# Key and query weights transposed by the DMA queues instead of TensorE, and late loads moved to GpSimd's queue

## The chip, the cores and the metric

The kernel runs on one core of a Trainium2 chip. The core has a matrix engine (TensorE, PE in the profile; its weight loads are listed as PEld), VectorE (DVE), ScalarE (ACT), GpSimd (POOL) and SyncE (SP), which here only issues transfers. Sixteen DMA engines move data between HBM and the on-chip memory SBUF; they are fed by queues that SP, ScalarE and GpSimd issue into. Matmul results go to PSUM, eight banks of 512 fp32 columns. The metric is the time of one execution on the device in microseconds (us); lower is better.

## The reference

A layer norm feeds two branches, which are added to the input: linear attention with a softmax feature map (32 heads of 16), and a gated feed-forward layer with GELU.

```python
# x: 1 x 2048 x 512, H = 32, Dh = 16, feed-forward width 1376, all bf16
def _A_ref(x, wqkv, w_phi, wo):
    qkv = (x @ wqkv) ...                      # split into q, k, v per head
    pq = einsum("bhsd,hdf->bhsf", q, w_phi)
    pk = einsum("bhsd,hdf->bhsf", k, w_phi)
    phi_q = concat([softmax(pq), softmax(-pq)])
    phi_k = concat([softmax(pk), softmax(-pk)])
    kv = einsum("bhsf,bhsd->bhfd", phi_k, v)
    z  = einsum("bhsf->bhf", phi_k)
    num = einsum("bhqf,bhfd->bhqd", phi_q, kv)
    den = einsum("bhqf,bhf->bhq", phi_q, z) + 1e-6
    return (num / den) ... @ wo
def _B_ref(x, w_gate, w_up, w_down):
    return (gelu(x @ w_gate) * (x @ w_up)) @ w_down
xn = layernorm(x)
return x + _A_ref(xn, ...) + _B_ref(xn, ...)
```

## The kernel before

**Tiling.** The 2048 tokens are 16 tiles of 128 (index t or r) and 4 chunks of 512 (index s). The normed input is kept transposed in `xnT`, channels on the partitions. The feed-forward width is 11 units (`NF`; ten of 128 and one of 96), index jf; `J = s*11 + jf`.

**Who decides the order.** Every instruction is first put down as an operation with its reads, writes and a cost in us (`op`, `alt`, `dma`). A list scheduler (`Sched.schedule`) then walks a model of the engines, always takes the ready operation with the lowest priority number, and so fixes one order per engine. That order is replayed with semaphore waits in front of each operation (`_replay`). On the chip an engine never goes past a waiting instruction: what stands behind it in the order waits too. A DMA belongs to the engine that issues it, so a DMA that waits for something stops that engine: SP, or GpSimd in the middle of its arithmetic. SP has 12 DMA semaphores and uses them in turn.

**The stages.**

1. Start: 11 spare matmuls on zeros, then token tiles 0 to 3: `ln_stats`, `ln_rstd` (on GpSimd) and `ln_norm` on VectorE write `xn_sb` (six buffers); `xt_pe` transposes them on TensorE, and `gate4` starts the gate projection of chunk 0.
2. Feed-forward chunk 0: for each unit, gate and up projections (`lin`, four 512-wide matmuls each, into banks 0 to 3), GELU on ScalarE and the product with up on VectorE (`glu`, into `hT`). The norms of tiles 4 to 7, 8 to 11 and 12 to 15 (`ln_group`) run beside it on VectorE, and `xt_dma` transposes each by a DMA that SP issues, SBUF to SBUF, into `xnT`.
3. Weight folding, also beside chunk 0: the key weights are loaded into a free part of `hT` (`wk_nat`), the query weights into a free part of `EqT` (`wq_nat`). `wtrans` transposes them in four groups of eight 128x128 TensorE transposes through PSUM, `wtrans_out` copies them to SBUF on ScalarE (`wkT`, `wqT`), and `fold` multiplies them with the block-diagonal `bd` made from `w_phi`, giving `wk2` and `wq2`. So pq and pk come straight from xn.
4. Projection phase over 16 token tiles: `proj_k` and `proj_q` (banks 0 to 2 in turn) with two exponentials each on ScalarE, into `Ek` and `EqT`; `proj_v` (banks 3 and 4). The sums of the exponentials, `Ssum`, are made by GpSimd in four steps (`st1`, `st2`, `st3`, `Ssum`), and by VectorE for tiles 3, 7, 11 and 15. `v_post` (VectorE) takes the reciprocal of the sums and scales the values; `kv_acc` (TensorE, "kv product of tile t" below) accumulates key features times scaled values in banks 5 to 7.
5. Chunks 1 to 3 of the feed-forward layer, with the attention (`att`) and the output tiles (`outp`, which uses `wo_sb` and `wd_sb`) in between.

**Loads.** SP issues nearly all of them, in the order: x tiles, gate and up weights, key weights, x 8 to 11, query weights, x 12 to 15, value weights. `gate_dma` is a list of transfers that a load has to wait for. `big_loads` issues wo and w_down from GpSimd, and waits for the last `xnT` transpose (`d_xt[15]`).

Of the kernel before, what the change touches and what calls it, by code (L numbers as in the profile page):

```python
# [7 lines left out]
ACTF = mybir.ActivationFunctionType  # L8
# [40 lines left out]
class Sched:  # L49
# [150 lines left out]
def bass_parallel_sum__linear_kernel_hedgehog__glu_gated_geglu__prompt_kernel(  # L200
# [14 lines left out]
    with ExitStack() as es, nc.allow_low_precision("bf16 softmax factors"):  # L215
# [10 lines left out]
        ident = sb([P, 128], bf16, "ident")  # L226
# [23 lines left out]
        wkT = hT[:, 1, 0:4, :]  # L250
        wk_nat = hT[:, 1, 4:8, :]
# [10 lines left out]
        wqT = EqT[:, 0:4, 1536:2048]  # L262
        wq_nat = EqT[:, 4:8, 1536:2048]
# [25 lines left out]
        def bank16(b):  # L289
            return bank(b).bitcast(bf16)  # L290
# [29 lines left out]
        B_wkn = bufs("wkn", 2)  # L320
        B_wqn = bufs("wqn", 2)
        B_wk2 = bufs("wk2", 4)
        B_wq2 = bufs("wq2", 4)
        B_wv = bufs("wv", 2)
# [25 lines left out]
        def load_x(q, t, n):  # L350
            return dma(q, lambda e: e.dma_start(
                x_all[:, t:t + n, :], x2[t * P:(t + n) * P, :].rearrange("(n p) c -> p n c", p=P)),
                writes=B_x[t:t + n], lat=1.9, kb=128 * n, prio=-900, extra=gate_dma)

        def load_w(dst, lo, bf, qs=("sp", "act")):
            v = A_wqkv[:, lo:lo + 512].rearrange("(i p) c -> p i c", p=P)
            for h, q in enumerate(qs):
                dma(q, lambda e, h=h: e.dma_start(dst[:, 2 * h:2 * h + 2, :], v[:, 2 * h:2 * h + 2, :]),
                    writes=[bf[h]], lat=1.9, kb=256, prio=-900, extra=gate_dma)

        def load_f(dst, src, c, bf, qs=("sp", "act")):
# [17 lines left out]
        dma("pool", lambda e: e.dma_start(  # L379
            wphi[:], A_w_phi.rearrange("(j hl) d f -> (hl d) j f", j=4)), writes=[B_wphi], cost=1.0, lat=4.0,  # L380
            prio=-900)
        load_x("sp", 8, 4)
        load_w(wq_nat, 0, B_wqn, ("sp", "sp"))
        load_x("sp", 12, 4)
        load_w(wv_sb, 1024, B_wv, ("sp", "sp"))


        op("dve", lambda e: e.memset(warm[:], 0.0), writes=[B_warm], cost=0.3, prio=-900)
# [51 lines left out]
        def proj_k(t, b):  # L440
            op("pe", [lambda e, i=i: e.matmul(  # L441
                bank(b), xnT[:, i, t * P:(t + 1) * P], wk2[:, i, :], start=(i == 0), stop=(i == 3))
                for i in range(4)], reads=[B_xnT[t]] + B_wk2, writes=[BK[b]], cost=mm(4))
            for sig in range(2):
                exps.append(op("act", lambda e, sig=sig: e.activation(  # L445
                    Ek[:, t, sig, :], bank(b), ACTF.Exp, scale=(1.0, -1.0)[sig]),
                    reads=[BK[b]], writes=[B_Ek[t][sig]], cost=0.55, extra=gelus, tab="exp"))
            ev = Ek[:, t, :, :].rearrange("p s (h f) -> p (s h) f", f=DH)
            if t in SDVE:
                op("dve", lambda e: e.tensor_reduce(Ssum[:, t, :], ev, axis=mybir.AxisListType.X, op=ALU.add),  # L450
                   reads=B_Ek[t], writes=[B_S[t]], cost=1.24)
# [8 lines left out]
            op("pool", lambda e: e.tensor_tensor(v3, v2[:, :, 0:2], v2[:, :, 2:4], op=ALU.add),  # L460
               reads=[B_st[1]], writes=[B_st[2]], cost=0.4, lock=True)
            op("pool", lambda e: e.tensor_tensor(Ssum[:, t, :], v3[:, :, 0], v3[:, :, 1], op=ALU.add),  # L462
               reads=[B_st[2]], writes=[B_S[t]], cost=0.29)
# [169 lines left out]
                   reads=[B_y[y], B_x[t]], writes=[B_ob[k]], cost=1.17, lock=True)  # L633
            dma("sp", lambda e: e.dma_start(out2[t * P:(t + 1) * P, :], ob[:, k, :]), reads=[B_ob[k]], writes=[], lat=1.3, kb=128)

        def wtrans(w, Bw, jj, b):
            op("pe", [lambda e, i=i, j=j: e.transpose(  # L637
                bank16(b)[:, (j % 2) * 512 + i * 128:(j % 2) * 512 + (i + 1) * 128],
                w[:, i, j * 128:(j + 1) * 128], ident[:]) for j in (2 * jj, 2 * jj + 1) for i in range(4)],
               reads=Bw + [B_ident], writes=[BK[b]], cost=mm(8, 128))  # L640

        def wtrans_out(wT, BwT, jj, b, extra=()):
            dst, src = wT[:, 2 * jj:2 * jj + 2, :], bank16(b).rearrange("p (j c) -> p j c", j=2)
            op("act", lambda e: e.activation(dst, src, ACTF.Copy), cost=1.0, reads=[BK[b]],
               writes=BwT[2 * jj:2 * jj + 2], extra=extra)

        def fold(wT, BwT, w2, B_w2, j, b):
            op("pe", [lambda e, i=i: e.matmul(  # L648
                bank(b)[:, i * 128:(i + 1) * 128], wT[:, j, i * 128:(i + 1) * 128], bd[:, j, :],
                start=True, stop=True) for i in range(4)], reads=[BwT[j], B_bd], writes=[BK[b]], cost=mm(4, 128))  # L650
            dst, src = w2[:, :, j * 128:(j + 1) * 128], bank(b).rearrange("p (i c) -> p i c", i=4)
            alt([("act", lambda e: e.activation(dst, src, ACTF.Copy), 0.55),
                 ("dve", lambda e: e.tensor_copy(dst, src), 0.69)], reads=[BK[b]], writes=[B_w2[j]])


        op("pe", [lambda e: e.matmul(bank(7), warm[:, 0:128], warm[:], start=True, stop=True) for _ in range(11)],  # L656
           reads=[B_warm], writes=[BK[7]], cost=4.2)
# [13 lines left out]
        def kq():  # L671
            turn[0] += 1
            return (turn[0] - 1) % 3
# [38 lines left out]
        for jf in range(4, NF):  # L712
            gelus.append(ffn(jf))
            if jf in (5, 8):
                ln_group({5: 8, 8: 12}[jf])
            if jf in (5, 6):
                wtrans(wk_nat, B_wkn + B_hT[1][4:8], jf - 5, 4 + jf % 2)
                wtrans_out(wkT, B_wkT, jf - 5, 4 + jf % 2)
            if jf in (7, 8):
                wtrans(wq_nat, B_wqn + B_Eq[3][4:8], jf - 7, 4 + jf % 2)  # L720
                wtrans_out(wqT, B_wqT, jf - 7, 4 + jf % 2)
            if jf == 7:
                for j in range(4):
                    fold(wkT, B_wkT, wk2, B_wk2, j, 6 + j % 2)
            if jf == 9:
                for j in range(4):
                    fold(wqT, B_wqT, wq2, B_wq2, j, 6 + j % 2)
        big_loads()


        LAG, KA = 3, 3
        nv = 0

        def val():
# [91 lines left out]
```

## Time and profile before

| | |
|---|---|
| three runs | 201.5, 201.76, 202.19 us (median 201.76) |
| profiled execution | 201.5 us, of which the span of its instructions is 199.7 |
| granted TensorE clock | 1.00 in every stretch |
| TensorE transposes of the weights (L637) | 4 groups of 8, first start 18.55 us |
| DMA transposes into xnT (L425) | 12, first issue 16.9, last issue 35.5 us; 2.4 to 6.7 us to landing |
| first use of wo (L616) | 91.1 us |

The span is counted from the first instruction to the last; all places in time below are from its start. Most of the kernel is the same stream of 512-wide matmuls; the change touches what happens in the first 60 us. DMA traffic by the page, in 40 slices of 5 us:

```profile
GB/s 167 333 377 346 187 103 60 61 299 86 0 0 0 3 0 0 0 28 28 26 53 53 31 53 26 26 49 33 26 26 56 26 30 51 26 54 28 53 26 54
```

The loads of x and of the weights fill the first five slices; the slices at 40 and 45 us are wo and w_down. In what follows a row of a timeline is: start, length, engine and line, operation, tiles, count, and in brackets the idle time before it and who ended it. A length covers all instructions that the row merges.

### The profile page before, as it was taken

The page shows a single profiled execution, that of the slowest core. Times are in us where ns is not written, and L with a number is a line of the kernel's source. Part 1 is how long each engine was busy: PE and PEld are TensorE (multiplying, and loading weights), DVE is VectorE, ACT ScalarE, POOL GpSimd, SP SyncE. Part 2 cuts the span into 40 slices and gives each one's busy share as a digit, 9 for nine tenths or more (in the row PEclk, how much of TensorE's full clock was granted, in tenths as well). Part 3 has the DMA queues.
Part 4 walks back from the last instruction along what each step waited for, and adds up shares of the span by engine and source line. Part 5 has one row for each costly group of instructions (what it writes and reads, how often), then busy time and mean ns, then how long its engine had stood idle before and what let it go on. Part 6 is the DMA issues. An engine that isn't in the chain of part 4 may idle for free.

```text
span 199.7 us, 3131 instructions
## 1 busy us (share of the span) xinstructions
PE 195.3 (98%) x1183; PEld 101.2 (51%) x1183; DVE 130.6 (65%) x297; ACT 81.4 (41%) x140; POOL 75.5 (38%) x105
## 2 busy tenths in 40 slices
PE   7999999999999999999999999999999999999994
PEld 2665665546555556555455555545545555454441
DVE  3788993549868576685986874959167494853121
ACT  2373798985676765343022222322223132222000
POOL 5630212999997820022432242342222324222100
PEclk9999999999999999999999999999999999999999
DMA  5999954282000000011022121041102102021101
GB/s 167 333 377 346 187 103 60 61 299 86 0 0 0 3 0 0 0 28 28 26 53 53 31 53 26 26 49 33 26 26 56 26 30 51 26 54 28 53 26 54
DMA packets 24079, 14.41 MB, mean 72 GB/s; under 512 B 15888, under 2 KB 23584, under 8 KB 24064
## 3 DMA queue, kind: packets, MB, share of 16 engines
q1 hardware_dynamic: 22944, 11.74, 23.7%
q0 software_dynamic: 560, 1.95, 2.9%
q10 hardware_dynamic: 560, 0.52, 0.8%
q8 instruction: 9, 0.15, 0.3%
q14 instruction: 6, 0.05, 0.1%
HBM read 8.44 MB, written 2.10 MB: 53 GB/s over the span
## 4 chain that ended last, share of the span: by engine, by line
PE 98%; DVE 0%; ACT 0%; issue 0%
PE ps_all L536 36%; PE ps_all L620 19%; PE ps_all L616 7%; PE ps_all L466 7%; PE ps_all L477 7%; PE ps_all L441 7%; PE ps_all L568 4%; PE ps_all L503 4%; PE ps_all L656 2%; PE ps_all L551 2%; PE ps_all L637 1%; PE ps_all L648 1%; PE ps_all L433 1%; DVE ob L626 0%; ACT xnT L437 0%; PE ps_all L664 0%
## 5 line engine op out<-in xcount | busy, mean ns | idle before, releaser
L536 PE MATMUL ps_all<-xnT,wu_sb 128*128 128x512 bf16 (+1 forms) x176 | 44.4, 379 | 0.0
L527 ACT ACTIVATE gs<-ps_all 128x512 bf16<-128x512 f32 (+1 forms) x44 | 25.9, 598 | 40.6 <-PE ps_all L536 37.7
L536 PE MATMUL ps_all<-xnT,wg_sb 128*128 128x512 bf16 (+1 forms) x160 | 40.7, 379 | 0.0
L620 PE MATMUL ps_all<-wd_sb,hT 128*128 128x512 bf16 (+1 forms) x176 | 40.6, 379 | 0.0
L608 POOL TENSOR_TENSOR o_sb<-otmp 128x512 bf16<-128x512 bf16 x16 | 18.4, 1153 | 55.6 <-DVE otmp L602 55.6
L529 DVE TENSOR_TENSOR hT<-gs,ps_all 128x512 bf16<-128x512 bf16 (+1 forms) x44 | 28.7, 679 | 14.5 <-PE ps_all L536 14.4
L620 PEld LDWEIGHTS ps_all<-wd_sb,hT 128*128 128x128 bf16 (+1 forms) x176 | 17.2, 98 | 20.8
L536 PEld LDWEIGHTS ps_all<-xnT,wu_sb 128*128 128x128 bf16 (+1 forms) x176 | 17.4, 100 | 19.0
L632 POOL TENSOR_TENSOR ob<-y_sb,x_all 128x512 bf16<-128x512 f32 x12 | 13.8, 1153 | 26.2 <-ACT y_sb L630 26.2
L630 ACT ACTIVATE y_sb<-ps_all 128x512 f32<-128x512 f32 x12 | 7.2, 597 | 40.0 <-PE ps_all L620 40.0
L536 PEld LDWEIGHTS ps_all<-xnT,wg_sb 128*128 128x128 bf16 (+1 forms) x160 | 15.3, 100 | 14.4
L602 DVE TENSOR_TENSOR otmp<-ps_all,cf 128x384 bf16<-128x384 f32 (+1 forms) x48 | 21.7, 507 | 0.5
L487 DVE TENSOR_TENSOR vs<-ps_all,vs 128x1024 bf16<-128x1024 f32 x16 | 19.4, 1217 | 3.4 <-PE ps_all L477 3.2
L445 ACT ACTIVATE Ek<-ps_all 128x512 bf16<-128x512 f32 x32 | 17.3, 610 | 8.1 <-PE ps_all L441 8.0
L472 ACT ACTIVATE EqT<-ps_all 128x512 bf16<-128x512 f32 x32 | 17.7, 619 | 5.1 <-PE ps_all L466 5.1
L585 DVE RECIPROCAL r_sb<-ps_all 128x48 f32<-128x48 f32 (+1 forms) x32 | 9.2, 327 | 13.5 <-PE ps_all L568 13.5
L484 DVE RECIPROCAL vs<-Ssum 128x64 bf16<-128x64 f32 x16 | 8.7, 554 | 12.3 <-POOL Ssum L462 12.2
L466 PE MATMUL ps_all<-xnT,wq 128*128 128x512 bf16 x64 | 16.4, 379 | 0.0
L616 PE MATMUL ps_all<-wo_sb,oT 128*128 128x512 bf16 x64 | 16.4, 379 | 0.0
L477 PE MATMUL ps_all<-wv_sb,xnT 128*128 128x512 bf16 x64 | 16.3, 379 | 0.0
L441 PE MATMUL ps_all<-wk,xnT 128*128 128x512 bf16 x64 | 16.1, 379 | 0.0
L456 POOL TENSOR_TENSOR st<-Ek 128x512 f32<-128x512 bf16 x12 | 13.9, 1154 | 5.3 <-ACT Ek L445 5.3
(64 smaller groups left out, 186.1 us busy)
## 6 DMA issues: line engine op xcount, KB each, us to landing
out_dram<-ob SPq DMA_DIRECT2D x16, 128.0 KB, 1.7
x_all<-in_A_x_dram SPq DMA_DIRECT2D x3, 512.0 KB, 9.8
wd_sb<-in_B_w_down_dram POOLq DMA_DIRECT2D x1, 1280.0 KB, 9.4
wg_sb<-in_B_w_gate_dram SPq DMA_DIRECT2D x2, 432.0 KB, 6.6
wu_sb<-in_B_w_up_dram SPq DMA_DIRECT2D x2, 432.0 KB, 7.7
wu_sb<-in_B_w_up_dram SPq DMA_DIRECT2D x2, 256.0 KB, 4.5
hT<-in_A_wqkv_dram SPq DMA_DIRECT2D x2, 256.0 KB, 8.6
EqT<-in_A_wqkv_dram SPq DMA_DIRECT2D x2, 256.0 KB, 9.6
```

What stands on the lines that cost most here:

```text
L441: op("pe", [lambda e, i=i: e.matmul(bank(b), xnT[:, i, t * P:(t + 1) * P], wk2[:, i, :], start=(i == 0), stop=(i == 3)) for i in range(4)] ...
L466: op("pe", [lambda e, i=i: e.matmul(bank(b), wq2[:, i, p * 128:(p + 1) * 128], xnT[:, i, s * 512:(s + 1) * 512], start=(i == 0), stop=(i = ...
L472: exps.append(op("act", lambda e, g=g, sig=sig: e.activation(EqT[:, g, s * 512:(s + 1) * 512], bank(b), ACTF.Exp, scale=(1.0, -1.0)[sig]), ...
L477: op("pe", [lambda e, i=i: e.matmul(bank(b), xnT[:, i, t * P:(t + 1) * P], wv_sb[:, i, :], start=(i == 0), stop=(i == 3)) for i in range(4 ...
L487: op("dve", lambda e: e.tensor_tensor(v[:, :, :, 0:DH], bank(b).rearrange("p (h d) -> p h d", d=DH).unsqueeze(1).to_broadcast([P, 2, 32, DH]),
L527: h = op("act", lambda e: e.activation(gs[0:w, k, :], bank(gb)[0:w, :], ACTF.Gelu_apprx_tanh), reads=[BK[gb]], writes=[B_gs[k]], cost=0.55 ...
L529: op("dve", lambda e: e.tensor_tensor(hT[0:w, s % 2, jf, :], gs[0:w, k, :], bank(ub)[0:w, :], op=ALU.mult), reads=[B_gs[k], BK[ub]], write ...
L536: op("pe", [lambda e, i=i: e.matmul(bank(b)[0:w, :], wt[:, i, jf * 128:jf * 128 + w], xnT[:, i, s * 512:(s + 1) * 512], start=(i == 0), st ...
L602: op("dve", lambda e, q=q, n=n: e.tensor_tensor(otmp[:, k, q * 384:q * 384 + n * 128].rearrange("p (s h d) -> p s h d", s=n, d=DH), bank(4 ...
L608: op("pool", lambda e: e.tensor_tensor(o_sb[:, k, :], otmp[:, k, 0:512], otmp[:, k, 512:1024], op=ALU.add), reads=B_ot[k], writes=[B_o[k]] ...
L616: fns = [lambda e, j=j: e.matmul(bank(b), oT[:, t % NOT, j, :], wo_sb[:, j, :], start=(j == 0), stop=False) for j in range(4)]
L620: fns.append(lambda e, jf=jf, w=w: e.matmul(bank(b), hT[0:w, s % 2, jf, tl * 128:(tl + 1) * 128], wd_sb[0:w, jf, :], start=False, stop=(jf ...
```

## The change

- `wtrans` no longer makes TensorE transposes; it has SP issue four DMA transposes per weight matrix (128x512 each, SBUF to SBUF), straight into `wkT` or `wqT`. `wtrans_out` is gone. The key weights' four are put down ahead of the norms of tiles 4 to 7, the query weights' four after them. Their priority places all eight on SP ahead of the xnT transposes of tiles 8 to 15.
- `fold` waits for all four DMA transposes of its matrix. The key folds use banks 4 to 7 and follow unit 7 of chunk 0. The query folds are moved from behind unit 9 into the projection phase, behind the first three `proj_k` (`KA` = 3, `FQ` = True).
- The query weights are loaded ahead of x 8 to 15. x 8 to 11, x 12 to 15 and the value weights are now issued by GpSimd: x 8 to 11 after the first half of the second part of the up weights has landed, the others after x 8 to 11 have landed.

```diff
-        load_x("sp", 8, 4)
         load_w(wq_nat, 0, B_wqn, ("sp", "sp"))
-        load_x("sp", 12, 4)
-        load_w(wv_sb, 1024, B_wv, ("sp", "sp"))
+        gate_dma = [B_wu[2].last_write]
+        load_x("pool", 8, 4)
+        gate_dma = [B_x[8].last_write]
+        load_x("pool", 12, 4)
+        load_w(wv_sb, 1024, B_wv, ("pool", "pool"))
...
-        def wtrans(w, Bw, jj, b):
-            op("pe", [lambda e, i=i, j=j: e.transpose(...) for j in (2 * jj, 2 * jj + 1) for i in range(4)],
-               reads=Bw + [B_ident], writes=[BK[b]], cost=mm(8, 128))
-        def wtrans_out(wT, BwT, jj, b, extra=()):
-            op("act", lambda e: e.activation(dst, src, ACTF.Copy), cost=1.0, reads=[BK[b]], ...)
+        def wtrans(w, Bw, wT, BwT):
+            for i in range(4):
+                dma("sp", lambda e, i=i: e.dma_start_transpose(wT[:, :, i * 128:(i + 1) * 128], w[:, i, :]),
+                    reads=[Bw[i // 2]] + Bw[2:], writes=[BwT[i]], cost=1.2, lat=1.4, kb=310)
...
         def fold(wT, BwT, w2, B_w2, j, b):
-            ... reads=[BwT[j], B_bd], writes=[BK[b]], cost=mm(4, 128))
+            ... reads=BwT[0:4] + [BwT[4 + j], B_bd], writes=[BK[b]], cost=mm(4, 128))
...
+        wtrans(wk_nat, B_wkn + B_hT[1][4:8], wkT, B_wkTi)
         ln_group(4)
+        wtrans(wq_nat, B_wqn + B_Eq[3][4:8], wqT, B_wqTi)
...
-            if jf in (5, 6):
-                wtrans(wk_nat, ...); wtrans_out(wkT, ...)
-            if jf in (7, 8):
-                wtrans(wq_nat, ...); wtrans_out(wqT, ...)
             if jf == 7:
                 for j in range(4):
-                    fold(wkT, B_wkT, wk2, B_wk2, j, 6 + j % 2)
-            if jf == 9:
+                    fold(wkT, B_wkTi + B_wkT, wk2, B_wk2, j, 4 + j)
+            if jf == 9 and not FQ:
...
         for r in range(KA):
             proj_k(r, kq())
+        if FQ:
+            for j in range(4):
+                fold(wqT, B_wqTi + B_wqT, wq2, B_wq2, j, (6, 7, 4, 5)[j])
```

As built, SP's order after the loads is: four transposes of the key weights, xnT 4 to 7, four of the query weights, xnT 8 to 15. In GpSimd's order the wo and w_down loads, which wait for xnT 15, now stand between the second and the third step of the sum of token tile 2 (before: between the first and second step of tile 1). TensorE's order in the projection phase begins k0, k1, v0, k2, the query folds, k3, k4, v1, q0, q1, kv 0, v2, k5, q2, kv 1, k6, q3, v3, k7, q4, k8, kv 2, v4, kv 3, q5, v5, kv 4.

More of the change, by code (lines that the diff above doesn't have):

```diff
@@ L320, in bass_parallel_sum__linear_kernel_hedgehog__glu_gated_geglu__prompt_kernel @@
         B_wkn = bufs("wkn", 2)
+        B_wkTi, B_wqTi = bufs("wkTi", 4), bufs("wqTi", 4)
         B_wqn = bufs("wqn", 2)
@@ L634, in outp @@
             dma("sp", lambda e: e.dma_start(out2[t * P:(t + 1) * P, :], ob[:, k, :]), reads=[B_ob[k]], writes=[], lat=1.3, kb=128)
-        def wtrans(w, Bw, jj, b):
-            op("pe", [lambda e, i=i, j=j: e.transpose(
-                bank16(b)[:, (j % 2) * 512 + i * 128:(j % 2) * 512 + (i + 1) * 128],
-                w[:, i, j * 128:(j + 1) * 128], ident[:]) for j in (2 * jj, 2 * jj + 1) for i in range(4)],
-               reads=Bw + [B_ident], writes=[BK[b]], cost=mm(8, 128))
-        def wtrans_out(wT, BwT, jj, b, extra=()):
-            dst, src = wT[:, 2 * jj:2 * jj + 2, :], bank16(b).rearrange("p (j c) -> p j c", j=2)
-            op("act", lambda e: e.activation(dst, src, ACTF.Copy), cost=1.0, reads=[BK[b]],
-               writes=BwT[2 * jj:2 * jj + 2], extra=extra)
+        def wtrans(w, Bw, wT, BwT):
+            for i in range(4):
+                dma("sp", lambda e, i=i: e.dma_start_transpose(wT[:, :, i * 128:(i + 1) * 128], w[:, i, :]),
+                    reads=[Bw[i // 2]] + Bw[2:], writes=[BwT[i]], cost=1.2, lat=1.4, kb=310)
         def fold(wT, BwT, w2, B_w2, j, b):
@@ L649, in fold @@
                 bank(b)[:, i * 128:(i + 1) * 128], wT[:, j, i * 128:(i + 1) * 128], bd[:, j, :],
-                start=True, stop=True) for i in range(4)], reads=[BwT[j], B_bd], writes=[BK[b]], cost=mm(4, 128))
+                start=True, stop=True) for i in range(4)], reads=BwT[0:4] + [BwT[4 + j], B_bd], writes=[BK[b]], cost=mm(4, 128))
             dst, src = w2[:, :, j * 128:(j + 1) * 128], bank(b).rearrange("p (i c) -> p i c", i=4)
@@ L653, in fold @@
                  ("dve", lambda e: e.tensor_copy(dst, src), 0.69)], reads=[BK[b]], writes=[B_w2[j]])
+        LAG, KA, FQ = 3, 3, True
         op("pe", [lambda e: e.matmul(bank(7), warm[:, 0:128], warm[:], start=True, stop=True) for _ in range(11)],
@@ L715, in bass_parallel_sum__linear_kernel_hedgehog__glu_gated_geglu__prompt_kernel @@
                 ln_group({5: 8, 8: 12}[jf])
-            if jf in (5, 6):
-                wtrans(wk_nat, B_wkn + B_hT[1][4:8], jf - 5, 4 + jf % 2)
-                wtrans_out(wkT, B_wkT, jf - 5, 4 + jf % 2)
-            if jf in (7, 8):
-                wtrans(wq_nat, B_wqn + B_Eq[3][4:8], jf - 7, 4 + jf % 2)
-                wtrans_out(wqT, B_wqT, jf - 7, 4 + jf % 2)
             if jf == 7:
                 for j in range(4):
-                    fold(wkT, B_wkT, wk2, B_wk2, j, 6 + j % 2)
-            if jf == 9:
+                    fold(wkT, B_wkTi + B_wkT, wk2, B_wk2, j, 4 + j)
+            if jf == 9 and not FQ:
                 for j in range(4):
-                    fold(wqT, B_wqT, wq2, B_wq2, j, 6 + j % 2)
+                    fold(wqT, B_wqTi + B_wqT, wq2, B_wq2, j, 6 + j % 2)
         big_loads()
-        LAG, KA = 3, 3
         nv = 0
```

## Prediction, made before the changed kernel was run

> **What bounds the kernel now.** I read the page's shares first, then the chain that ended last, then the timelines of each engine over the first 60 us, the only stretch where the diff acts.
>
> ```profile
> PE 195.3 (98%) x1183; PEld 101.2 (51%) x1183; DVE 130.6 (65%) x297; ACT 81.4 (41%) x140; POOL 75.5 (38%) x105
> PE 98%; DVE 0%; ACT 0%; issue 0%
> ```
>
> TensorE is busy for 98% of the span and is 98% of the chain. So a TensorE instruction taken away is worth its full spacing, and a pause put into TensorE costs its full length.
>
> ```profile
> 15.10 1.03 PE L536 MATMUL ps_all<-xnT,wg_sb 128*128 128x512 bf16 x4
> 18.55 0.61 PE L637 MATMUL ps_all<-ident,hT 128*128 128x128 bf16 x8
> 19.00 1.03 PE L536 MATMUL ps_all<-xnT,wg_sb 128*128 128x512 bf16 x4
> 30.76 2.75 PE L441 MATMUL ps_all<-wk,xnT 128*128 128x512 bf16 x12
> ```
>
> Columns: start, length, engine and line, then the work. Eight transposes take 19.00-18.55 = 0.45 us of TensorE, and none of these rows has an idle note. By 15.10 TensorE starts unit 4 of chunk 0; at 30.76 it starts the key projections.
>
> ```profile
> 7.38 1.00 SPq L358 DMA_DIRECT2D hT<-in_A_wqkv_dram  x2
> ...
> 16.95 6.22 SPq L425 DMA_TRANSPOSE xnT<-xn_sb  x4
> 24.37 6.03 SPq L425 DMA_TRANSPOSE xnT<-xn_sb  x4
> 31.62 5.12 SPq L425 DMA_TRANSPOSE xnT<-xn_sb  x4
> 35.52 1.21 SPq L425 DMA_TRANSPOSE xnT<-xn_sb  x1
> DMA to landing us min/median/max: 8.0/8.6/9.3
> ```
>
> This is SP's timeline; the last line is the landing time of the two key-weight loads (first row), so the first half lands at 7.38+8.0 = 15.4. Three of the last four transposes take 5.12-1.21 = 3.91 us, that is, SP issues one DMA transpose per 1.30 us. Each lands 2.43 us after its issue (the smallest of the twelve, 2.4 to 6.7).
>
> ```profile
> 38.26 0.85 POOL L687 DMA_DIRECT2D wo_sb<-in_A_wo_dram  x1
> 39.11 0.98 POOL L690 DMA_DIRECT2D wd_sb<-in_B_w_down_dram  x1
> 40.08 0.56 POOL L693 DMA_DIRECT2D wd_sb<-in_B_w_down_dram  x1
> ...
> 41.47 0.40 POOL L460 TENSOR_TENSOR st<-st 128x128 f32<-128x128 f32 x1
> 41.95 0.29 POOL L462 TENSOR_TENSOR Ssum<-st 128x64 f32<-128x64 f32 x1
> ```
>
> GpSimd issues the wo and w_down loads itself, between two steps of a softmax sum. They wait for the last xnT transpose (35.52+2.43 = 37.95), which in this kernel is there when GpSimd arrives.
>
> ```profile
> 45.04 0.56 DVE L484 RECIPROCAL vs<-Ssum 128x64 bf16<-128x64 f32 x1 [0.94 <-POOL Ssum L462]
> 45.63 2.36 DVE L487 TENSOR_TENSOR vs<-ps_all,vs 128x1024 bf16<-128x1024 f32 x2
> 47.91 1.21 DVE L450 TENSOR_REDUCE Ssum<-Ek 128x64 f32<-128x1024 bf16 x1
> 49.03 0.55 DVE L484 RECIPROCAL vs<-Ssum 128x64 bf16<-128x64 f32 x1
> 49.62 1.23 DVE L487 TENSOR_TENSOR vs<-ps_all,vs 128x1024 bf16<-128x1024 f32 x1
> ```
>
> VectorE waits for GpSimd's sum of token tile 2, and then works 49.62+1.23-45.04 = 5.81 us without a gap until the value tile 4 is scaled. TensorE's kv product of tile 4 needs that tile.
>
> **The change part by part.** *Removed:* 32 transposes on TensorE, 4 groups of 0.45 us (0.445 unrounded), together **-1.78 us**, all on the chain. Four ScalarE copies (1.02 us each) go too; TensorE never waits for ScalarE in these rows, so they are worth nothing.
>
> *Without any new wait* TensorE would go: 15.10 + 7 units of 1.73 (eight 512-wide matmuls, from 19.00 to the next group's start at 20.73) = 27.2; key folds 0.89 (two groups of eight, 0.445 each); then, in the order that the changed kernel is built with, 21 projections of 0.864, the query folds 0.89 and four kv products of 0.475 before the kv product of tile 4: 27.2+0.89+18.14+0.89+1.90 = **49.0**. (0.864 is half of 1.73; 0.475 is the step from a kv product, 66.10, to what follows, 66.57.) The same walk puts the key folds at 22.0, the query folds at 31.5, kv 0 at 36.8 and kv 2 at 45.5.
>
> *Added:* eight DMA transposes on SP, all in the same queue as the twelve of xnT: four of the key weights first, then xnT 4 to 7, four of the query weights, xnT 8 to 15. The first one waits for the key load, 15.4. Before, the last of the twelve started at 35.52; now twenty in a row, bound by SP. The twentieth starts no earlier than 15.4 + 19 x 1.30 = 40.1 and lands at 42.5. Three unknowns stand beside this. The pace: with every start-to-start at the shortest pair seen, 1.23, landing is at 41.3. A hiccup: the middle four took 6.03 us instead of 5.12, so +0.9, and over twenty issues I count one. A full queue: the first four took 6.22 us under the loads, +1.1; if the fifth is not taken until the first has landed, and that comes as late as 25 (before: 16.95+6.7 = 23.6, behind the value weights), the slip is 25-22 = 3; bounds 0 and 3, I take 0.5, half of the 1.1, as only the value weights and x 12 to 15 are left beside them. Landing: 42.5+0.9+0.5 = **43.9**, bounds 41.3 and 46.4.
>
> [...] The rows give 1.30 us of issue each, and the sum goes by them.
>
> *The wait and what stands behind it.* GpSimd's order now has the wo load, still waiting for the last xnT transpose, between the second and third step of the sum of tile 2. GpSimd gets there at about 38 to 40, and stands until 43.9. Behind it: 0.1 to wake, 2.40 for three issues (38.26 to 40.66), 0.77 for two steps of the sum (41.47 to 42.24): tile 2's sum is done at 43.9+3.3 = 47.2, not before 42. VectorE's five instructions take 5.81, with 0.1 for semaphores: kv 4 can start at 53.1, that is **4.1 late**. (kv 2, after reciprocal and product, 1.9 us: 49.1 against 45.5, 3.6 late.) From there sums come every 2.77 us (42.20 to 44.96 before) for three tiles in four, and TensorE needs 3.07 per tile (63.04 to 66.10), so nothing later is later still.
>
> *Other new waits* end on the same TensorE, so the largest counts and not the sum. Key folds: fourth key transpose, start 19.3, landing 21.7 at best and 25 if starved, 0 to 3 late. Query folds: twelfth transpose, 15.4+11x1.30+2.43+1.4 = 33.5 against 31.5, 2.0 late. kv 0: VectorE stands in order at the norm of tile 15 until xnT 9 has freed its buffer, 15.4+13x1.30+2.43+1.4 = 36.1; plus norm 0.4, reciprocal and product 1.9, 38.4 against 36.8, 1.6 late. All are below 4.1.
>
> *Moved:* x 8 to 15 and the value weights to GpSimd's queue, three loads later by a wait each. x 8 starts when the up weights land (13.5). The bytes are the same, and the page's slices from 10 to 20 us already run at 377 and 346 GB/s, so x 8 lands near 18 to 20, against 18.7. VectorE's products for TensorE stand behind it, at most 1 us late, again below 4.1. wo and w_down land near 56 (43.9+2.4+9.4, the longest landing of the three before); the first use is at 91: hidden.
>
> **Sum.** +4.1-1.78 = +2.3. The profiled execution took 201.5 us (span 199.7), the lowest of 201.5, 201.76 and 202.19; 201.5+2.3 = 203.8 by it, 204.1 by the median. Forecast **203.9**. With the bounds of the landing: 41.3 gives 1.5-1.78, so 201.2; 46.4 gives 6.6-1.78, so 206.3.
>
> A pause matters twice if the clock falls. Every stretch here has a granted clock of 1.00 and no pause. [...]
>
> **Rivals.** (a) *Forecast:* SP's chain of twenty holds GpSimd; 202.2 to 205.2. For: the fixed order and 1.30 us. Chance 0.61.
> (b) *Starved transposes:* the software queue's loads keep the key transposes back to 25, the queue fills, landing at 46: 201.5-1.78+46.1-39.8 = 206.0. For: the 6.7 us landing; against: fewer loads than before. 0.15.
> (c) *No change:* no hiccup and no slip, landing 41.0 to 42.2, lateness 1.2 to 2.4 against 1.78 saved: about 201.5. Against: 1.23 was the shortest pair, never a run. 0.14.
> (d) *Faster, the other side:* the twenty land before anybody asks, and only the 1.78 remains: 199.7. Lateness is landing minus 39.8, so it decides from a landing below 41.0 (0.3% off) and is whole at 39.8, at a pace of 1.16. For: 8 x 1.30 us is little against 1183 matmuls; against: the shortest single issue is 1.19. 0.10.
>
> A difference of 0.3%, 0.6 us, is what this kernel's measurement can tell. Below -0.3% is (d), 0.10; within, (c), 0.14; above, (a) and (b), 0.76. Range 201.3 to 206.0: (c), (a) and most of (b); (a)'s own is 202.2 to 205.2.
>
> **What would show it.** Right: no transposes on TensorE; twenty SP transposes at 1.3 us from 15.4 to about 41; GpSimd idle near 39 to 44, released by a DMA into xnT; TensorE idle some 4 us between 22 and 54, last at a kv product. Wrong: GpSimd not idle there, TensorE unbroken, transposes closer than 1.2 us, or a granted clock below 1.

## The result, and the profile after

| | before | after |
|---|---|---|
| median of the runs | 201.95 us (201.5 to 202.19, 4 runs) | 204.64 us (204.53 to 205.48, 4 runs) |
| profiled execution, of which span | 201.5, 199.7 us | 204.53, 202.8 us |
| TensorE transposes of the weights | 32 | 0 |
| first idle note of TensorE after 15 us | none | 23.20 us, four in all |
| last matmul starts at | 196.40 us | 199.23 us |

The ratio is 1.0145, with a 95% interval of 1.0111 to 1.0178: the change costs 2.7 us. The granted clock is 1.00 in every stretch up to the last matmul. Four executions of the experiments below (205.63 to 210.08 us) ran at a lower granted clock (0.983 to 0.992), and the medians and ratios leave them out.

The page's shares and its chain that ended last, after the change:

```profile
PE 193.5 (95%) x1151; PEld 99.0 (49%) x1151; DVE 131.3 (65%) x298; ACT 77.3 (38%) x135; POOL 78.7 (39%) x109
PE 77%; DMA 10%; DVE 5%; SPq 4%; POOL 2%; issue 1%
```

TensorE is busy 193.5 us instead of 195.3, so the 1.8 us of transposes did go. But the chain is 77% TensorE, where it was 98%: the rest passes through SP's queue (SPq), transfers (DMA), GpSimd and VectorE. TensorE's timeline, the rows with an idle note between 15 and 54 us:

```profile
23.20 1.07 PE L645 MATMUL ps_all<-bd,hT 128*128 128x128 bf16 x16 [1.03 <-DMA hT<-hT]
39.29 0.65 PE L506 MATMUL ps_all<-vs,Ek 128*128 128x136 bf16 x8 [1.18 <-DVE vs L490]
49.61 0.65 PE L506 MATMUL ps_all<-vs,Ek 128*128 128x136 bf16 x8 [1.43 <-DVE vs L490]
53.60 0.59 PE L506 MATMUL ps_all<-vs,Ek 128*128 128x136 bf16 x7 [0.28 <-DVE vs L490]
```

In the order of time these are the key folds, released by a transpose of the key weights, and the kv products of token tiles 0, 2 and 4, released by VectorE. The notes come to 3.9 us. A note counts from the modelled end of the matmul before it, some 0.16 us late; from start to start the four cost 1.20, 1.34, 1.60 and 0.44, together 4.6 us. SP's timeline, and below it the summary of the line that issues the xnT transposes (durations, then landing times):

```profile
15.36 5.20 SPq L641 DMA_TRANSPOSE hT<-hT  x4
20.66 5.24 SPq L428 DMA_TRANSPOSE xnT<-xn_sb  x4
25.95 5.41 SPq L641 DMA_TRANSPOSE EqT<-EqT  x4
31.45 11.56 SPq L428 DMA_TRANSPOSE xnT<-xn_sb  x8
```

```profile
L428 SPq DMA_TRANSPOSE xnT<-xn_sb x12: 1210/1260/2430, 20.7 to 41.7; - x12
...
DMA to landing us min/median/max: 2.5/3.4/5.5
```

Twenty transposes in a row keep SP issuing without a break: the first at 15.36, the last at 41.74. The median one takes 1.26 us, one took 2.43, and from start to start it is about 1.3 in most places. The chain of waits, walked back by the profile from TensorE's work at 56 us and shown in the order of time (start, length, what):

```profile
23.20 1.07 PE ps_all L645 x16
...
32.76 4.30 DMA xnT<-xn_sb
37.06 0.03 issue
37.09 0.41 DVE xn_sb L422
...
41.74 2.53 DMA xnT<-xn_sb
44.27 0.29 issue
44.56 0.83 POOL wo_sb L685
45.39 0.00 issue
45.39 0.96 POOL wd_sb L688
46.35 0.55 POOL wd_sb L691
...
47.41 0.30 POOL Ssum L465
...
48.33 2.36 DVE vs L490 x2
...
53.60 0.65 PE ps_all L506 x8
```

It reads: the twentieth transpose is issued at 41.74 and lands at 44.27; only then does GpSimd get past the wo load, which takes it with the two w_down loads to 46.9; only then the sum of tile 2; then VectorE's chain; then TensorE. How long GpSimd and VectorE stood is in their own timelines:

```profile
44.56 0.83 POOL L685 DMA_DIRECT2D wo_sb<-in_A_wo_dram  x1 [4.51 <-DMA xnT<-xn_sb]
47.73 0.56 DVE L487 RECIPROCAL vs<-Ssum 128x64 bf16<-128x64 f32 x1 [5.18 <-POOL Ssum L465]
```

GpSimd idle for 4.51 us in front of a load that nobody needs before 94 us, and VectorE idle for 5.18 us behind it.

From the kv product of tile 15 on, TensorE runs the same stream in both kernels: it starts at 81.03 before and at 83.86 after, and from there to the last matmul both take 115.38 us. So the change is over at about 54 us, and its price there is 83.86-81.03 = 2.83 us: 1.78 saved, 4.61 late. The span grew by 3.04. The remaining 0.2 lies behind the last matmul (3.34 us before, 3.56 after).

### The profile page after: what moved, and what is told of

Same layout as the page of the kernel before. It is cut to its first block, busy times and chain, and to the rows that moved or that the text cites. A ratio compares the mean times of both kernels' runs of the same rounds, so it can differ in the third digit from the quotient of the medians.

```text
span 202.8 us, 3076 instructions
## 1 busy us (share of the span) xinstructions
PE 193.5 (95%) x1151; PEld 99.0 (49%) x1151; DVE 131.3 (65%) x298; ACT 77.3 (38%) x135; POOL 78.7 (39%) x109
## 4 chain that ended last, share of the span: by engine, by line
PE 77%; DMA 10%; DVE 5%; SPq 4%; POOL 2%; issue 1%
PE ps_all L539 31%; PE ps_all L623 19%; PE ps_all L619 7%; PE ps_all L480 5%; PE ps_all L469 4%; PE ps_all L444 4%; PE ps_all L571 4%; DMA hT<-in_A_wqkv_dram 4%; DMA xnT<-xn_sb 3%; PE ps_all L506 3%; DVE vs L490 2%; DMA hT<-hT 2%; SPq L641 2%; SPq L366 2%; DMA x_all<-in_A_x_dram 1%
```

## The experiments

Four runs use the kernel's own DMA transposes. In the other eight every DMA transpose is an ordinary copy of the same 128 KB between the same tiles. They leave the transposition out and keep the numbers and sizes of the rest, so that the pace of the issues can be set apart from the transposing. The start of an execution shifts its places by some 1 us (unit 4 of chunk 0 starts at 14.90 us with the paced copies below and at 15.92 with all waits moved and copies at their own pace); where runs are compared, it is by the time from unit 4 of chunk 0 to the kv product of tile 15, which is 65.93 us in the kernel before (15.10 to 81.03) and 68.76 in the changed one (15.10 to 83.86). Each ratio is to runs of the kernel before on the same chip (medians 202.0, 201.81 and 202.11 us).

**The output weights' loads on SP.** If GpSimd's standing is the price, another issuer for the three loads takes it away and leaves the transposes as they are.

```diff
 def big_loads():
-    dma("pool", lambda e: e.dma_start(wo_sb[:], ...), cost=1.0, ...)
-    dma("pool", ... wd_sb ...)   # twice
+    dma("sp", lambda e: e.dma_start(wo_sb[:], ...), cost=0.8, ...)
+    dma("sp", ... wd_sb ...)     # twice
```

> The changed kernel, with the wo and w_down loads issued by SP behind the last xnT transpose, and not by GpSimd. Theory (GpSimd stands at these loads until 44.3 and keeps the sums of tile 2 and later back): GpSimd's 4.5 us idle and the pauses before kv 2 and kv 4 (1.43 and 0.28 us) go. What is left is TensorE's lateness at kv 0, 39.29 against 36.75 = 2.5, less the 1.78 saved: 0.8 us above before, about 202.7 against 201.95, ratio 1.004; last pause on TensorE at kv 0. Rival (the twenty transposes and the loads of the software queue slow the core by themselves, the place of the wait is incidental): no gain, 204.5, ratio 1.013.

202.70 us, ratio 1.0030 [1.0011, 1.0049], 1.94 us less than the changed kernel. SP's and TensorE's rows of this run:

```profile
44.33 0.39 SPq L685 DMA_DIRECT2D wo_sb<-in_A_wo_dram  x1
```

```profile
24.42 1.04 PE L539 MATMUL ps_all<-xnT,wu_sb 128*128 128x512 bf16 x4 [0.26 <-DVE hT L532]
31.14 1.04 PE L480 MATMUL ps_all<-wv_sb,xnT 128*128 128x512 bf16 x4 [0.51 <-DVE hT L532]
39.23 0.65 PE L506 MATMUL ps_all<-vs,Ek 128*128 128x136 bf16 x8 [0.97 <-DVE vs L490]
42.30 0.64 PE L506 MATMUL ps_all<-vs,Ek 128*128 128x136 bf16 x8
45.36 0.64 PE L506 MATMUL ps_all<-vs,Ek 128*128 128x136 bf16 x8
48.43 0.64 PE L506 MATMUL ps_all<-vs,Ek 128*128 128x136 bf16 x8
```

The twentieth transpose lands at 44.3, as late as before the edit, and still the kv products now follow each other every 3.06 us without a pause. A late transpose by itself cost TensorE nothing there; the load waiting on GpSimd did. From unit 4 to the kv product of tile 15 it is 66.43 us (15.30 to 81.73), 2.33 less than in the changed kernel; only 0.26 of this was gained ahead of kv 0. The three pauses left come to 2.24 us from start to start (1.74 by the notes), which is more than the gain of 1.78.

**The early pauses out, GpSimd left as it is.** Ten layer-norm buffers for six (VectorE no longer stands at tile 15), and the key folds one unit later. A sum of all pauses as the price would make this faster by about 2 us; the largest one alone would hide the others.

```diff
-NXN = 6
+NXN = 10
...
-            if jf == 7:      # key folds
+            if jf == 8:
```

> The changed kernel with ten buffers for the normed tiles in place of six (VectorE needn't stand until xnT 8 and 9 have freed one) and the key folds one unit later. So the two early pauses of TensorE, 1.03 and 1.18 us, lose their cause; GpSimd's wait for the last transpose stays. Theory (waits on one engine count by the largest lateness, not by their sum): the early pauses shrink to 0.3 or less and come back before kv 2, which grows from 1.43 to 3.5 to 4.1 us, as tile 2's sum still comes at 47.7; kv 4 now has a projection more in front of it, so its 0.3 to 0.5 goes. Time 204.1 to 204.6, ratio 1.011 to 1.013. Rival (each pause has its own price): 1.03 + 1.18 less, 202.4, ratio 1.002. [...]

204.53 us (202.84, 204.53 and 204.62), ratio 1.0101 [1.0055, 1.0146]. The median is that of the changed kernel, as it should be if the last wait swallows the early ones. The profile fell on the shortest of the three, whose 202.84 us by itself would also suit the rival. But in it SP's twenty issues had no long one, the twentieth transpose landed at 43.09 and kv of tile 2 started at 48.42, against 44.27 and 49.61 in the changed kernel: 5.33 and 5.34 us behind the landing. The earlier landing (1.18 us) and the pause before kv 4 that is gone (0.44) make 1.6 of the 1.69 us between the two profiled executions. The key folds still waited 0.36 us by the note, kv 0 no longer did, and the pause before kv 2 grew to 1.68, not to the 3.5 to 4.1 expected. The other two executions have no profile, so that their landing was as late as in the changed kernel is not shown.

**The moved loads alone.** The kernel before, with x 8 to 15 and the value weights on GpSimd's queue as in the change.

```diff
-load_x("sp", 8, 4); load_w(wq_nat, ...); load_x("sp", 12, 4); load_w(wv_sb, 1024, B_wv, ("sp", "sp"))
+load_w(wq_nat, ...)
+gate_dma = [B_wu[2].last_write]; load_x("pool", 8, 4)
+gate_dma = [B_x[8].last_write];  load_x("pool", 12, 4); load_w(wv_sb, 1024, B_wv, ("pool", "pool"))
```

> The kernel before with one part of the change: the query weights ahead of x 8 to 15, and x 8 to 15 and the value weights issued by GpSimd behind their waits. The TensorE transposes stay. Theory (the bytes are the same and these loads have slack): x 8 lands near 19.5 and x 12 near 24, twelve SP transposes end near 38 to 39, no new pause on TensorE over 0.3 us; 201.6 to 202.4, ratio 0.998 to 1.002. Rival (the later loads are what costs): 1 to 2 us slower, ratio 1.005 to 1.010, with pauses of TensorE before the norms' consumers.

202.68 us, ratio 1.0035 [1.0022, 1.0048]: a miss, 0.7 us instead of none. TensorE has no new pause, and from unit 4 to the kv product of tile 15 it takes 65.93 us (15.59 to 81.52), as before. Of the 0.7, 0.46 lies behind the last matmul (3.80 us there, 3.34 before), and 0.25 outside the span (time less span: 1.99 against 1.75). Neither is a wait of the first 60 us.

**All three edits, and the query weights' transposes ahead of xnT 4 to 7.**

> The changed kernel with wo and w_down issued by SP, ten buffers for the normed tiles, the key folds one unit later, and the query weights' four transposes ahead of xnT 4 to 7. Theory: with all four waits gone the 1.78 us of TensorE transposes are won, less about 0.3 at the key folds: 200.2 to 200.6 against 201.95, ratio 0.992 to 0.994, TensorE without a pause over 0.4 us after 7 us. Rival (twenty transposes by DMA leave a cost of their own somewhere else, in memory or in a later stage): 201.5 or above, with TensorE's rows longer or a pause in a place not named here.

202.28 us (201.71 to 203.73), ratio 1.0017 [0.9987, 1.0047]: a miss; not distinguishable from the kernel before. TensorE's rows:

```profile
20.34 1.04 PE L539 MATMUL ps_all<-xnT,wu_sb 128*128 128x512 bf16 x4 [0.40 <-DVE hT L532]
25.13 0.84 PE L645 MATMUL ps_all<-bd,hT 128*128 128x128 bf16 x12 [1.17 <-DMA hT<-hT]
36.03 1.04 PE L444 MATMUL ps_all<-wk,xnT 128*128 128x512 bf16 x4 [0.31 <-ACT Ek L448]
```

The waits of kv are gone and others have come: 1.88 us in all by the notes, again the whole gain. The key folds wait although they stand a unit later. Their fourth transpose was issued at 20.37, 0.24 before the loads of x 12 to 15 and, behind them, of the value weights; it landed at 25.08, 4.7 us later, where 2.5 is the least.

**The kernel before and the changed kernel with copies.** These two tell whether the price goes with the pace at which SP issues.

```diff
-e.dma_start_transpose(xnT[:, :, t*P:(t+1)*P], xn_sb[:, k, :])
+e.dma_start(xnT[:, :, t*P:(t+1)*P], xn_sb[:, k, :].rearrange("p (i c) -> p i c", i=4))
```

and in the same way for `wkT`, `wqT` and the transposes of the attention output.

> The kernel before, with each of its 28 DMA transposes replaced by an ordinary copy of the same 128 KB from SBUF to SBUF, same places, same waits (the transposition is left out). It is the base for the next runs. Theory (in the kernel before nothing on TensorE waits for these transposes): same time as before, 201.4 to 202.6, ratio 0.997 to 1.003. It also shows the start of a run on this chip: first up projection at 11.9 to 12.4 if the 0.7 us of the run with only the loads moved were the start, 11.6 to 11.7 if they were the moved loads.

> The changed kernel, with each of its 36 DMA transposes replaced by an ordinary copy of the same 128 KB (the transposition is left out); every order and every wait is as in the changed kernel. Theory (the price is SP's 1.3 us per transpose, 20 in a row): a copy is issued in 0.4 to 0.6 us, the twentieth lands before 40, GpSimd doesn't stand at the wo load, TensorE's pauses before kv 0, 2 and 4 go, and of the 1.78 us saved 0 to 0.6 are lost at the key folds: 200.2 to 201.0, ratio 0.991 to 0.996. Rival (number and bytes of the transfers, or the moved loads, cost, whatever the pace of SP): 203.5 or above, ratio over 1.007.

Before: 202.02 us, ratio 1.0003 [0.9992, 1.0014]; so its transposes cost it nothing. Changed: 201.05 us, ratio 0.9962 [0.9950, 0.9973], 3.6 us less than with transposes. The line of the xnT copies, GpSimd's load and TensorE's only noted pause in the changed kernel with copies:

```profile
L428 SPq DMA_DIRECT2D xnT<-xn_sb x12: 593/598/1318, 18.8 to 36.4; - x12
...
DMA to landing us min/median/max: 2.3/3.7/5.9
```

```profile
39.73 0.83 POOL L685 DMA_DIRECT2D wo_sb<-in_A_wo_dram  x1
```

```profile
31.28 1.04 PE L480 MATMUL ps_all<-wv_sb,xnT 128*128 128x512 bf16 x4 [0.32 <-DVE hT L532]
```

In the median a copy took SP 0.598 us to issue, a transpose 1.260. The least landing times are near each other, 2.3 and 2.5 us. So here the transposes were dear at the issue, not in the transfer. With copies the twentieth lands at 38.69, before GpSimd asks (39.73), and GpSimd doesn't stand. From unit 4 of chunk 0 to the kv product of tile 15, TensorE takes 64.84 us (80.72-15.88) against 65.93 in the kernel before with copies (81.65-15.72): 1.09 of the 1.78 us are kept. The other 0.69 are the pause shown, 0.48 from start to start, and 0.20 before an up projection at 24.74, too short for a note.

**The copies at the transposes' pace.** The first attempt put two copies of 4 KB ahead of each early copy, the second one.

```diff
+def slow_sp(src, reads):
+    for _ in range(2):            # second attempt: range(1)
+        dma("sp", lambda e: e.dma_start(pad[:, m, :], src), reads=reads, ...)
...
+            slow_sp(xn_sb[:, k, 0:16], [B_xn[k]])
             return dma("sp", lambda e: e.dma_start(xnT[...], xn_sb[...]) ...)
```

> The kernel of the run before this one, with two copies of 4 KB in front of each of the twenty early ones, so that SP needs some 1.3 us for each again, without any transposition. Theory (SP's pace alone decides): the twentieth lands at 42 to 46, GpSimd stands at the wo load until then, and TensorE's pauses before kv 0, 2 and 4 are back: 203.4 to 206, ratio 1.007 to 1.020. [...]

> The changed kernel with plain copies for transposes, and one small copy (4 KB, about 0.65 us of issue as the run with two of them showed) ahead of each early one, so that a pair takes about 1.3 us of SyncE's sequencer, the pace of the transposes. Queue theory: the twentieth early copy lands between 42 and 45 us, GpSimd stands 3 to 5 us at its output-weight load before it, kv of tile 2 starts 5.3 us behind that landing (47.3 to 50.3), and the time is 203 to 205 us, ratio 1.005 to 1.016, against 0.996 for the same copies at their own pace. Rival, that it is the transposing itself (its traffic or its landing) and not the pace of the issues that costs: 200.8 to 201.6 us, ratio 0.995 to 0.999, with no pause of GpSimd over 1 us.

Two small copies overshot: the two took SP 1.11 to 1.29 us and most large ones 0.62, so the pace became 2.0 us and not 1.3, and the time 220.86 us, ratio 1.0928 [1.0901, 1.0955]. One small copy: 206.06 us, ratio 1.0203 [1.0184, 1.0222], 1 us above what was expected; the last copy landed at 45.86 instead of 42 to 45. GpSimd's load in the run with one, and TensorE's rows at the key folds and around the kv product of tile 2:

```profile
46.15 0.83 POOL L695 DMA_DIRECT2D wo_sb<-in_A_wo_dram  x1 [2.02 <-DMA xnT<-xn_sb]
```

```profile
26.14 1.89 PE L655 MATMUL ps_all<-bd,hT 128*128 128x128 bf16 x16 [3.48 <-DMA hT<-hT]
...
50.04 1.03 PE L453 MATMUL ps_all<-wk,xnT 128*128 128x512 bf16 x4
51.19 0.65 PE L515 MATMUL ps_all<-vs,Ek 128*128 128x136 bf16 x8
```

Here are the four runs in which GpSimd stands at the load, set side by side:

| kernel | twentieth lands | kv of tile 2 starts | difference | from there to kv of tile 15 |
|---|---|---|---|---|
| changed | 44.27 | 49.61 | 5.34 | 34.25 |
| early pauses out | 43.09 | 48.42 | 5.33 | 33.79 |
| copies, one small copy | 45.86 | 51.19 | 5.33 | 34.24 |
| copies, two small copies | 58.14 | 63.47 | 5.33 | 35.41 |

Behind the landing of the twentieth the chain takes the same 5.33 us, whether or not the twenty transpose. In the run with two small copies TensorE stood 5.85 us before kv 2: a slow row of issues alone, without any transposing, brings the wait back.

The run with one small copy says less. Its key folds waited 3.48 us and its clock was halved for 3.4 us around the end of that (last section), so TensorE was some 5.6 us late by itself: the key projection ahead of kv 2 starts at 50.04 and takes 0.86, and kv 2 could have started at 50.90. GpSimd's load held it only to 51.19, and kv 4 0.44 us more. In this execution the load's place added 0.7 us, and most of the time above the kernel with unpaced copies came from the key folds. The other three executions show a mean granted clock of 1.00, against 0.992 in the profiled one, so no such halving, and took 206.05 to 206.09 us, no less than the profiled one (205.87). That suits a time set by the landing, but they have no profile.

The rival, that it is the transposing and not the pace, would have had this run near 201 us; it took 206 without any transposing. Whether transposing costs something besides is better read from the two kernels with the output weights on SP, the first experiment and the next one.

**The paced copies, with the output weights' loads on SP.** The edit of the first experiment upon this kernel.

> The paced copies with the output and down weights' three loads issued by SyncE instead of GpSimd. Queue theory: GpSimd no longer stands, kv of tile 2 and 4 follow without a pause, and the twentieth copy still lands at 42 to 45 us; what is left is the pauses ahead of it (key folds about 1, first kv about 1, worth 1 to 2 us in all against the gain of 1.78): 201.5 to 203 us, ratio 0.998 to 1.005. Rival, that TensorE waits for late copies as such and GpSimd's standing is only beside it: as the paced run with the loads on GpSimd, within 0.3 us.

202.96 us, ratio 1.0055 [1.0036, 1.0073]: 3.1 us less, and the kv products follow every 3.06 us (42.72, 45.78, 48.84, 51.91), though the last copy lands at 45.50. The rival (within 0.3 us of the kernel with the loads on GpSimd) is refuted by these rows. The 3.1 us aren't the price of GpSimd's standing alone, since in this run the key folds hardly waited either (0.12 us): the key weights came earlier (first copy issued 0.67 us behind the start of unit 4, against 2.25). What remains is pauses ahead of kv 2, 1.01 us at the first value projection the largest. From unit 4 to the kv product of tile 15 it is 66.61 us, against 66.43 with real transposes and the same loads on SP (first experiment), and the intervals of the two ratios overlap: no cost of the transposing beyond its pace is seen.

**Every wait found moved away**, with paced copies and with copies at their own pace: the three edits above, x 12 to 15 and the value weights held until the key weights' copies have landed, two layer-norm groups one unit later, the query folds behind the fourth key projection.

```diff
-        gate_dma = [B_x[8].last_write]
-        load_x("pool", 12, 4); load_w(wv_sb, 1024, B_wv, ("pool", "pool"))
         wtrans(wk_nat, B_wkn + B_hT[1][4:8], wkT, B_wkTi)
+        gate_dma = [B_wkTi[3].last_write]
+        load_x("pool", 12, 4); load_w(wv_sb, 1024, B_wv, ("pool", "pool"))
...
-            if jf in (5, 8):
-                ln_group({5: 8, 8: 12}[jf])
+            if jf in (6, 9):
+                ln_group({6: 8, 9: 12}[jf])
...
-        if FQ: ...                # query folds ahead of the loop over r
         for r in range(NT):
             if r + KA < NT:
                 proj_k(r + KA, kq())
+            if r == 0: ...        # query folds
```

> The paced copies with every wait found moved out of the way: output and down weights on SyncE's queue, ten layer-norm buffers for six, the later x tiles and value weights held until the key weights' copies have landed, the key folds and the two later layer-norm groups one projection later, the query folds behind the first key projection. If the pauses are each a late operand and nothing more, TensorE has under 0.5 us of pauses from 15 us to kv of tile 4 and the time is 200.3 to 201.3 us, ratio 0.992 to 0.997. Rival, that each pause taken out comes back at the next gate (as with the real transposes, where the query folds' order moved it to the key folds): 202 us or more, ratio above 1.0.

> As the run before with the copies at their own pace (no small copies). If the 0.69 us that the plain copies left of the gain are the pauses at the value projections and before the key projections: 200.2 to 200.8 us, ratio 0.991 to 0.995. Rival, that they are not pauses that order can take out: 201.0 to 201.6 us as the unpaced changed kernel, or above where the held loads come late for the value projections.

203.24 us, ratio 1.0064 [1.0043, 1.0086], and 203.01, ratio 1.0063 [1.0043, 1.0084]: both missed, and the rival of each held. TensorE's rows of the second:

```profile
32.34 1.90 PE L441 MATMUL ps_all<-wk,xnT 128*128 128x512 bf16 x8 [0.41 <-DVE hT L529]
37.01 1.04 PE L477 MATMUL ps_all<-wv_sb,xnT 128*128 128x512 bf16 x4 [1.01 <-ACT wq L646]
```

The waits came back elsewhere: the held x tiles land at 27.5, VectorE does their statistics up to 31.5, and its product of the last unit (`hT`) behind them is late; the query folds' results, copied out by ScalarE (`wq`), now hold the value projection that comes next. With the output weights on SP the pace matters little: 0.23 us between the two. The same copies without these moves (201.05 us) are better than with them.

**The moved loads alone, with copies.**

> The kernel before with only the loads moved, and its 28 DMA transposes replaced by ordinary copies (the transposition is left out). Theory (moved loads cost nothing): equal to the kernel before with ordinary copies, within 0.3 us, and the same start of the up projections within 0.2 us. Rival: 0.4 to 0.7 us above it, as the run with only the loads moved was 0.35% above before.

202.81 us, ratio 1.0044 [1.0029, 1.0059], 0.79 above the kernel before with copies: the theory missed. The first up projection starts at 12.37, and at 12.27 in the kernel before with copies, so that the late start in the third experiment (12.35) is not from the moved loads. TensorE's rows agree with that kernel's to 0.1 us up to the last matmul (197.13 and 197.02), while behind it lie 3.80 and 3.34 us. The third experiment showed the same, so the 0.46 belongs to the moved loads. The 0.25 outside the span is there again (1.98 against 1.73); what it is stays open.

Not tried with real transposes: the key weights alone by DMA (sixteen in a row), the later loads held back until the key weights are transposed, and all waits moved at once. No kernel here that computes the whole reference beats the kernel before: the best one is at 1.0017 with an interval that includes 1.

## Why the prediction was right

**The sum.** Forecast 203.9, measured 204.64; by its own execution 203.8 against 204.53. The direction, the mechanism and the place held; the 0.7 us between them consist of 0.5 at kv 4 and 0.2 behind the last matmul.

**-1.78 us.** TensorE's count fell by 32 and its busy time by 1.8. Shown.

**SP's pace.** 1.30 us per transpose was right: the four groups start at 15.36, 20.66, 25.95 and 31.45, thus 1.32, 1.32 and 1.38, and in the last eight 1.30 but for one issue. The mis-sized terms: the hiccup, counted at 0.9, was 2.43-1.26 = 1.17; the half us for a full queue was spent instead on the slightly slower first twelve, (31.45-15.36)-12x1.30 = 0.5. Landing 44.27 against 43.9. (The lower bound given for it, 15.4+19x1.23+2.43, is 41.2 and not 41.3; the forecast doesn't rest on it.) Part of this is luck. The first transpose had landed at 20.15, before the fifth was issued at 20.66, so a full queue had no chance to show: no run shows this term, and its half us fitted something else. And the hiccup is not there in every execution: the longest issue was 1.79 us with the loads on SP and 1.33 with the early pauses out, whose profiled time was 202.84.

**GpSimd, VectorE, kv.** The sum of tile 2 was done at 47.7 (47.2 predicted; the 0.1 to wake, which came from no row, was 0.29, from 44.27 to 44.56), kv 2 started at 49.61 (49.1), kv 4 at 53.60 (53.1): 4.6 late instead of 4.1. Moving the loads to SP removed the pauses at kv 2 and 4 and moved kv 0 by only 0.26; the paced copies brought GpSimd's standing back without any transposing.

**"The largest counts and not the sum."** Taking the early pauses out left the median where it was, by three executions of which one is 1.7 us shorter. The paced copies show where the rule ends: an early pause of 3.48 us, with the half clock after it, made TensorE nearly as late as the last wait, 0.29 us short of it at kv 2.

**The other waits.** Key folds 1.2 late (23.20 against 22.0; 0 to 3 predicted). The query folds were said to be 2.0 late; the twelfth transpose landed at 32.61, and TensorE, late from the key folds, reached them at 32.74: no pause. kv 0 was 2.5 late (39.29 against 36.8), not 1.6: VectorE got past tile 15's norm at 37.1 instead of 36.1, since the fourteenth transpose too came later. All stayed under the last wait, as the prediction had it; once that is gone they are what eats the gain.

**Moved loads.** x 8 landed at 19.5 (18 to 20 predicted), the last of w_down at 55.2 (56): hidden. "The bytes are the same" was right for TensorE, but the time behind the last matmul was not in the working: 0.2 us here, 0.46 with the loads alone.

**The rivals.** Starved transposes (b) didn't occur in the form priced, 25 us for the key weights; they landed at 23.15. (d), the faster side, needed a landing below 41.0, and a pace of 1.16 for the whole gain. The copies went through that door: at 0.6 us per issue they landed at 38.7 and the time was 201.05. Its price, 199.7, was too good by about 1 us: 0.7 of the gain went to pauses ahead of kv even then, and 0.2 lay behind the last matmul.

**Issue, transfer and clock.** In the transfer, transposes and copies differed little (least landing 2.5 us against 2.3), in the issue on SP by a factor of two (1.26 us against 0.60), and it was the issue that bound this kernel. No pause of the changed kernel was longer than 1.43 us by the notes, and its clock stayed at 1.00. With the paced copies the clock was halved around the pause of 3.48 us (last section), and the sixteen key folds behind it took 1.89 us, against 1.07 in the changed kernel.

## What to carry to other kernels

A load with a wait, put into the order of an engine that also computes, stops everything behind it (here GpSimd stood for 4.51 us): ask of each added transfer which engine's last wait hangs on it, and let an engine issue the load that has nothing to compute (from SP, 1.94 us less). Price moved DMA work by the issuing queue's time per instruction and its place in the queue, not by bytes alone: here 128 KB cost SP 0.60 us as a copy and 1.26 as a transpose. Where several waits end on the same bound engine, find the last one first; taking it out shows the next, and the gain of a change is only what is left after all of them.

## What the runs showed of the hardware that wasn't expected

**The clock after a pause.** TensorE's granted clock in stretches of the paced copies, with the pause of 3.48 us before 26.14 (columns: stretch, length, TensorE's busy time and count, granted clock, DMA share, GB/s), and then of the copies with two small ones, with pauses of 5.47 us before 28.98 and 5.85 before 63.47:

```profile
22.00:25.00 3.00, 0.66 (x4) 1.00 1.00 267
25.00:29.00 4.00, 2.86 (x20) 0.57 1.10 231
29.00:40.00 11.00, 11.00 (x64) 1.00 0.46 99
```

```profile
29.00:33.00 4.00, 4.00 (x23) 0.54 0.39 72
33.00:60.00 27.00, 21.75 (x123) 1.00 0.33 65
60.00:67.00 7.00, 3.53 (x21) 0.51 0.86 275
```

By the trace's clock records the clock was halved for 3.4 us (25.45 to 28.87) around the pause of 3.48 us, and for 6.8 us (25.88 to 32.71, 60.02 to 66.84) around those of 5.47 and 5.85; each time it fell before the pause was over. Noted pauses up to 1.84 us, in these and all the other profiles, left it at 1.00. No profile has a pause between 1.84 and 3.48. The other three executions of the run with one small copy show a mean of 1.00, and how long their pause was is not recorded.

**A small copy cost the issuer as much as a large one**: in the run with one small copy medians of 0.58 to 0.64 us of SP for 4 KB, by tile, and 0.62 for the 128 KB copies into xnT.

**Transfers beside a large load landed late in some runs.** In the paced copies the fourth key-weight copy was issued at 21.20, 0.65 us after the load of x 12 to 15 (20.55), and landed 4.9 us later. With the output weights on SP it was issued at 20.26, 0.47 us ahead of that load (20.73), and landed after 2.5 us. So the key folds waited 3.48 us in the one and had no noted pause in the other. The order of the issues alone doesn't decide it: in the changed kernel the fourth key transpose was issued 0.52 us ahead of that load (19.30 and 19.82) and took 3.9 us, with 2.5 the least.

**The end of the kernel.** Behind the last output transfer SP goes through a row of semaphore waits, 0.06 to 0.10 us apart in the kernel before. By the trace's semaphore records, in the kernel before the long one (for the last output) is the last of nine and ends 2.89 us after the last matmul's start; with the loads moved alone and copies it is the second of ten, ends at 2.88, and eight more follow it, 0.06 each. That is the 0.46 us; in the changed kernel four follow, and it is 0.21. The row goes through SP's transfer semaphores from the highest number down; the last output's is 104 in the kernel before and 108 in the changed one.
